# A fused gated-recurrence and two-layer kernel: moving first-unit copies between engines and merging the chunk-decay exponentials

## The chip, the cores and the metric

The kernel runs on one core of one Trainium2 chip. The metric is the device time of one execution in microseconds (us), as the median of several executions. The core has five engines with queues of their own: TensorE (PE, matmuls), VectorE (DVE), ScalarE (ACT), GpSimd (POOL) and SyncE (SP, which here only issues transfers), and 16 DMA engines. Each engine works through its own queue in order and waits on semaphores. In what follows, "Z", "X", "W", "H" and "O" are tensors in PSUM, the memory into which TensorE writes.

## The reference

First a gated linear recurrence over 768 tokens, for 4 batches and 8 heads of width 48; then a two-layer network on the 3072 resulting rows of 384 numbers, with a squared ReLU between its layers.

```python
def _attn_ref(q, k, v, alpha):                 # all (4, 8, 768, 48), float32
    state = np.zeros((B, H, D, D))
    for t in range(S):
        state = alpha[:, :, t, :, None] * state + np.einsum('bhd,bhde->bhde', k[:, :, t], v[:, :, t])
        y[:, :, t] = np.einsum('bhd,bhde->bhe', q[:, :, t], state)

def _moe_ref(x, w_in, w_out):                  # (3072, 384), (384, 2048), (2048, 384)
    r = np.maximum(x @ w_in, 0.0)
    return (r * r) @ w_out

x = attn_out.transpose(0, 2, 1, 3).reshape(B * S, H * D)
```

## The kernel before

The sequence is cut into chunks of 256 tokens; a chunk of one batch is a **unit**. There are 12 units, and units 0 to 3 are the first chunks of the four batches. A unit goes through these steps:

- **front**: load alpha, k, q and v; take logarithms of alpha on ScalarE; sum them along the tokens with a triangular matrix on TensorE; exponentials of the sums and of their negatives (ScalarE) give the decays `EQ` and `EK`; VectorE multiplies q and k by them (`QKS`); the result is transposed (`KQT`), for units 0 to 2 by TensorE through PSUM, and from unit 3 on by a transfer. The values are cast to bfloat16 (`VBF`).
- **kv** and **state**: products of keys and values (TensorE), masked to a head's own block (`SMD`), and carried to the next chunk with the chunk's decay (`SBD`).
- **p** (scores, 32 small matmuls), a mask (`PM`, VectorE), and **y** (output of the unit); then a copy to bfloat16 (`XBF`), a transpose (`XT`), and the two-layer network: first layer (`s1`, 48 matmuls of 256 columns in eight groups of six), ReLU, square, second layer (`s2`, 32 matmuls of 384 columns).

The instructions are not written in queue order. The kernel records operations with a priority (`prio`), a modelled cost and, where there is a choice, alternatives (`alts`) on another engine. A list scheduler in the same file then picks engine and order when the program is built. So a change of a number changes the order in all queues. Where the modelled TensorE queue has a hole ahead of the first second-layer matmul, `fill` puts matmuls of zeros there, into a bank whose content nobody reads.

The parts that the change touches (cuts are marked with `...`):

```python
    # which load is issued behind which (gates)
    AFTER = {(1, "v"): (0, "q"), ("win", 0): (1, "a"), ("win", 1): (1, "a"), 2: ("win", 0), ("wout", 0): ("win", 1),
             ("wout", 1): (2, "k"), 3: ("wout", 0)}
    ...
    # unit 0 only: front in two halves of four heads
    add("act", ... activation(ACM[la][:, 4 * x:4 * x + 4], bank[:, HD:HD + 4], AF.Exp), ..., name=f"ec{x}_{g}")
    add("pool", lambda e: e.tensor_copy(vout, vin), 830, p0 + 900, reads=[("raw", r, 3)], writes=[("vbf", vb)],
        name=f"vc{g}", alts={"act": (lambda e: e.activation(vout, vin, AF.Copy), act_ns(2 * HD))})
    ...
    add("dve", lambda e, to=to, at=at: e.tensor_copy(to, at), dve_ns(512, 2), px + 3000 + a, reads=psk,
        writes=[("kqt", kt, a, x)], name=f"et{a}{x}_{g}",
        alts={"act": (lambda e, to=to, at=at: e.activation(to, at, AF.Copy), act_ns(512))})
    ...
    # units 2 to 11: decays of pairs of tokens
    add("act", ... e.activation(EK[la][:, 1, :], psW[:, 0:HD], AF.Exp, scale=-1.0), ..., name=f"ei{g}")
    add("act", ... e.activation(EQ[la][:, 1, :], psW[:, 0:HD], AF.Exp), ..., name=f"ea{g}")
    if not last:
        add("act", ... e.activation(ACM[la][:], psW[:, HD:HD + H], AF.Exp), ..., name=f"ec{g}")
    ...
    # state: mask to the head's own block (first chunks), then the decay to the next chunk
    if first:
        add("dve", lambda e: e.tensor_tensor(sm3, hd(ps0), own, ALU.mult), dve_ns(HD), p0 + 2900,
            reads=[key0, ("own",)], writes=[("smd", x2)], name=f"sa{g}")
    ...
    if not last:
        acm = bcast(ACM[la], H, [[1, H], [0, D]])
        add("dve", ... tensor_tensor(TMP[1][:], ps1, SMD[x2][:], ALU.add), ..., name=f"sc{g}")
        add("pool", ... tensor_tensor(hd(SBD[sw][:]), hd(TMP[1][:]), acm, ALU.mult), ..., name=f"sd{g}",
            alts={"dve": ...})
```

Of the kernel before, what the change touches and what calls it, by code (L numbers as in the profile page):

```python
# [321 lines left out]
def act_ns(n):  # L322
    return 180 + n * 0.8333


def dve_ns(n, rate=1.0):
    return 150 + n / 0.96 / rate
# [6 lines left out]
def bass_gla_recurrent__then__act_relu_squared_kernel(  # L334
# [22 lines left out]
    FRONT = {0: 0, 1: 15124, 2: 28243, 3: 27962, 4: 36918, 5: 52460}  # L357
    ATTN = {1: 12619, 2: 26150, 3: 37152, 4: 50460}
    DENSE = {0: 20223, 1: 32105, 2: 46275, 3: 57124, 11: 158500}
    POOL_LOADS = {1: "v", 2: "akqv"}  # L360
# [16 lines left out]
    EQ = sb("eq", [128, 2, HD], FP32, 2)  # L377
    EK = sb("ek", [128, 2, HD], FP32, 2)
    ACM = sb("acm", [128, H], FP32, 2)
# [23 lines left out]
    OWN = nc.alloc_sbuf_tensor("own", [128, H], BF16)  # L403
    ZERO = nc.alloc_sbuf_tensor("zero", [128, 512], BF16)
# [40 lines left out]
    for buf, key in ((HSEL, "hsel"), (HCOL, "hcol"), (OWN, "own")):  # L445
        add("dve", fill(buf[:], 0.0), 100, -2e6, writes=[(key,)])
    for part, key, val in ((HSEL[0:1, 64:128], "hsel", -1000.0), (HSEL[32:33, 0:64], "hsel", -1000.0),
                           (HCOL[0:1, 0:H:2], "hcol", 1.0), (HCOL[32:33, 1:H:2], "hcol", 1.0),
                           (OWN[0:64, 0:H:2], "own", 1.0), (OWN[64:128, 1:H:2], "own", 1.0)):
        add("dve", fill(part, val), 100, -2e6, reads=[(key,)], writes=[(key,)])  # L450
# [20 lines left out]
    def weight(lay, w):  # L471
        cut = slice(w * FS * 128, (w + 1) * FS * 128) if lay == 0 else slice(w * FS, (w + 1) * FS)
        if lay == 0:
            src, dst = moe_w_in.rearrange("(kk p) n -> p kk n", p=128)[:, :, cut], WIN[:, :, cut]
        else:
            src = moe_w_out[w * FS * 128:(w + 1) * FS * 128, :].rearrange("(p e) n -> p (e n)", e=FS)
            dst = WOUT[:, cut, :].rearrange("p e n -> p (e n)")
        key = ("win", "wout")[lay]
        load_op[key, w] = add("pool", lambda e: e.dma_start(dst, src), 930, W_PRIO[lay] + w, writes=[(key, w)], name=f"{key}{w}",
                              dma=f"{key}{w}", lag=8600 / WS,  # L480
                              after=[load_op[AFTER[key, w]]] if (key, w) in AFTER else [])

# [4 lines left out]

    def named(x):
        return next(o for o in pr.ops if o.name == x)

    BEHIND = {"a": "ln", "k": "tr0_", "q": "tr1_", "v": "tr1_"}

    def load(g):
        b, i = units[g]
        t0 = i * T
        p0 = g * P
        r, la, qs, kt, pm, vb, x2 = (g % n for n in (NRAW, 2, NQKS, NKQT, NPM, NV, 2))
        first, last = i == 0, i == NST - 1
        sr, sw = 2 * b + i % 2, 2 * b + (i + 1) % 2

        for x in range(2) if g in BY_HEADS else ():
            hs = slice(4 * x, 4 * x + 4)
            src = alpha[b, hs, t0:t0 + T, :].rearrange("h (p j) d -> p h (j d)", j=2)
            dst = RAW[r][:, 0, hs].rearrange("p h j d -> p h (j d)")
            add("sp", lambda e, dst=dst, src=src: e.dma_start(dst, src), 600, L_PRIO[g] + x * 0.5,  # L505
                writes=[("raw", r, 0, x)], name=f"lda{x}_{g}", dma=f"a{r}{x}", lag=615)
        for j, t, nm in ((0, alpha, "a"), (1, k, "k"), (2, q, "q"), (3, v, "v"))[g in BY_HEADS:]:
            src = t[b, :, t0:t0 + T, :].rearrange("h (p j) d -> p h (j d)", j=2)
            dst, key = RAW[r][:, j], ("raw", r, j)
            ring, cost, gate = "sp", 600, AFTER.get((g, nm), AFTER.get(g))  # L510
            if nm in POOL_LOADS.get(g, ""):
                ring, cost = "pool", 930
            dst = dst.rearrange("p h j d -> p h (j d)")
            load_op[g, nm] = add(ring, lambda e, dst=dst, src=src: e.dma_start(dst, src), cost, (L_PRIO[g] + j if ring == "sp" else W_PRIO[2] + 10 * g + j),  # L514
                writes=[key], name=f"ld{nm}{g}", dma=f"{nm}{r}{ring}", lag=1230,
                after=([load_op[gate]] if gate else []) + ([named(f"{BEHIND[nm]}{g - 1}")] if g >= 5 else []))

    def front_by_heads(g, p0):
# [4 lines left out]
        def lanes(t, x):  # L523
            return t[la][:].rearrange("p j (x n) -> p j x n", x=2)[:, :, x]

        for x in range(2):
# [25 lines left out]
            add("act", lambda e, x=x, sums=sums: e.activation(lanes(EK, x), sums, AF.Exp, scale=-1.0), act_ns(HD),  # L552
                px + 500, reads=key, writes=[("ek", la, j, x) for j in range(2)], name=f"ei{x}_{g}")
            add("act", lambda e, x=x, sums=sums: e.activation(lanes(EQ, x), sums, AF.Exp), act_ns(HD),
                px + 510, reads=key, writes=[("eq", la, j, x) for j in range(2)], name=f"ea{x}_{g}")
            add("act", lambda e, x=x, bank=bank: e.activation(ACM[la][:, 4 * x:4 * x + 4], bank[:, HD:HD + 4], AF.Exp),
# [4 lines left out]
            name=f"vc{g}", alts={"act": (lambda e: e.activation(vout, vin, AF.Copy), act_ns(2 * HD))})  # L561

        for x in range(2):
            hs = slice(4 * x, 4 * x + 4)
            px = p0 + 40 * x
            for a, E, nm in ((0, EK, "ek"), (1, EQ, "eq")):
                add("dve", lambda e, a=a, E=E, hs=hs, x=x: e.tensor_tensor(
                    QKS[qs][:, a, :, hs, 0:D], RAW[r][:, 1 + a, hs].rearrange("p h j d -> p j h d"),
                    lanes(E, x).rearrange("p j (h d) -> p j h d", h=4), ALU.mult), dve_ns(HD), px + 1500 + 10 * a,
                    reads=[("raw", r, 1 + a, x), (nm, la, 0, x), (nm, la, 1, x)], writes=[("qks", qs, a, x)], name=f"{nm}m{x}_{g}")  # L570
            for a in range(2):
                bank, psk = psZ[:, a, :].bitcast(BF16), [("ps", "Z", a)]

                def tr(pe, a=a, bank=bank, hs=hs):
# [11 lines left out]
                add("dve", lambda e, to=to, at=at: e.tensor_copy(to, at), dve_ns(512, 2), px + 3000 + a, reads=psk,  # L586
                    writes=[("kqt", kt, a, x)], name=f"et{a}{x}_{g}",
                    alts={"act": (lambda e, to=to, at=at: e.activation(to, at, AF.Copy), act_ns(512))})

    def decays_by_token(g, p0, r, la):  # L590
# [22 lines left out]
        add("act", lambda e: e.activation(EQ[la][:], bank[:, 0:2, 0:HD], AF.Exp), act_ns(2 * HD), p0 + 510,  # L613
            reads=keys, writes=[("eq", la, 0), ("eq", la, 1)], name=f"ea{g}")
        add("act", lambda e: e.activation(ACM[la][:], bank[:, 0, HD:HD + H], AF.Exp), act_ns(8), p0 + 520,
            reads=keys, writes=[("acm", la)], name=f"ec{g}")

    def decays_by_pair(g, p0, r, la, last):
# [11 lines left out]
        def m1(incl):  # L630
# [15 lines left out]
        add("act", lambda e: e.activation(EQ[la][:, 1, :], psW[:, 0:HD], AF.Exp), act_ns(HD), p0 + 510,  # L646
            reads=[("ps", "W")], writes=[("eq", la, 1)], name=f"ea{g}")
        if not last:
            add("act", lambda e: e.activation(ACM[la][:], psW[:, HD:HD + H], AF.Exp), act_ns(8), p0 + 520,
                reads=[("ps", "W")], writes=[("acm", la)], name=f"ec{g}")  # L650
# [4 lines left out]
        if g < RATIO:  # L655
            add("pe", m1(False), pe_ns(1, HD), p0 + 530, reads=[("lab", la), ("lstr",)], writes=[("ps", "W")],
                name=f"m1s{g}")
            add("act", lambda e: e.activation(EQ[la][:, 0, :], psW[:, 0:HD], AF.Exp), act_ns(HD), p0 + 540,
                reads=[("ps", "W")], writes=[("eq", la, 0)], name=f"es{g}")
            add("pool", lambda e: e.tensor_tensor(hd(EQ[la][:, 0, :]), hd(EQ[la][:, 0, :]), al(0), ALU.mult), pool_ns(HD),  # L660
                p0 + 800, reads=[("eq", la, 0), ("raw", r, 0)], writes=[("eq", la, 0)], name=f"aq{g}",
                alts={"dve": (lambda e: e.tensor_tensor(hd(EQ[la][:, 0, :]), hd(EQ[la][:, 0, :]), al(0), ALU.mult),
                              dve_ns(HD))})
            return
# [5 lines left out]
        add("act", lambda e: e.activation(EQ[la][:, 0, :], LA1[la][:], AF.Exp), act_ns(HD), p0 + 540,  # L670
            reads=[("la1", la)], writes=[("eq", la, 0)], name=f"es{g}")

    def front(g):
# [19 lines left out]
        for a, E, key in ((0, EK, "ek"), (1, EQ, "eq")):  # L693
            add("dve", lambda e, a=a, E=E: e.tensor_tensor(  # L694
                QKS[qs][:, a, :, :, 0:D], RAW[r][:, 1 + a].rearrange("p h j d -> p j h d"),
                E[la][:].rearrange("p j (h d) -> p j h d", h=H), ALU.mult),
# [85 lines left out]
    def state(g, alone=True):  # L782
# [10 lines left out]
        if first:  # L793
            add("dve", lambda e: e.tensor_tensor(sm3, hd(ps0), own, ALU.mult), dve_ns(HD), p0 + 2900,
                reads=[key0, ("own",)], writes=[("smd", x2)], name=f"sa{g}")
# [6 lines left out]
        if not last:  # L802
            acm = bcast(ACM[la], H, [[1, H], [0, D]])
            add("dve", lambda e: e.tensor_tensor(TMP[1][:], ps1, SMD[x2][:], ALU.add), dve_ns(HD),  # L804
                p0 + 3600, reads=[key1, ("smd", x2)], writes=[("tmp", 1)], name=f"sc{g}")
# [175 lines left out]
    W_PRIO = (-5e5, -4e5, -4.5e5)  # L981
    ORDER = ["f0", "k0", "p0", "f1", "y0", "p1", "k1", "y1", "f2", "p2", "k2"]
    for g in range(3, G):
        ORDER += [f"f{g}", f"w{g - 1}", f"p{g}"]
    ORDER += [f"y{G - 1}"]
    AFTER = {(1, "v"): (0, "q"), ("win", 0): (1, "a"), ("win", 1): (1, "a"), 2: ("win", 0), ("wout", 0): ("win", 1),
             ("wout", 1): (2, "k"), 3: ("wout", 0)}
    AFTER.update({g: (g - 1, "q") for g in range(4, G)})
    load(0)
    load(1)  # L990
    for w in range(WS):
        weight(0, w)
    load(2)
    for w in range(WS):
        weight(1, w)
    for st in ORDER:
        kind, g = st[0], int(st[1:])
        if kind == "f":
            if g > 2:
                load(g)  # L1000
# [41 lines left out]
```

## Time and profile before

The median of three executions is 179.0 us (178.62 to 179.14). The profiled execution has a span of 177.2 us; times below are from its start.

| What | Value | Where it is read |
|---|---|---|
| TensorE granted clock | 1.0 | result of the profiled run |
| VectorE, ScalarE, GpSimd busy | 121.1, 120.0, 26.2 us | page, part 1 |
| first-layer matmuls | 576, on the chain 38% of the span | page, parts 5 and 4 |
| second-layer matmuls | 368 of 384 columns and 32 of 192 | page, part 5, and the chain |
| matmuls of zeros | 72, of which 65 ahead of the first first-layer matmul | page, part 5; groups of 0 to 18.46 us |
| first first-layer matmul | 18.46 us | chain, timeline |
| last matmul ends | 174.77 us | chain |

The page has six parts. Part 1 sums the busy time of each engine; part 2 cuts the span in 40 slices and gives the busy share of each in tenths; part 4 is the chain that ended last, followed backwards from the last instruction, so its shares say what the time was spent on; part 5 lists groups of instructions with the mean of one; part 6 lists transfers. A TensorE that shows as busy isn't necessarily doing useful work: the matmuls of zeros count as busy, and so does a matmul that overlaps its neighbour. For that reason the prediction reads TensorE from the chain, where each piece is given once, and not from the busy sum.

### The profile page before, as it was taken

To read this page: it belongs to the slowest core of one execution; us is meant where nothing else is said; L and a number is where in the kernel's file an instruction comes from. 1 tells how busy PE (TensorE), PEld (TensorE's weight loads), DVE (VectorE), ACT (ScalarE), POOL (GpSimd) and SP (SyncE) were. 2 spreads that over 40 slices of the span, in tenths; PEclk is the share of its full clock that TensorE was granted. 3 is DMA by queue.
4 is the path that set the end of the run, shared out by engine and by line. 5 is a ranking of instruction groups with operands and counts; after the bars stand their busy time and mean duration, and the time that the engine had idled before them with its cause. 6 is when DMAs were issued, how large, how long until landed. Compare 5 with 4: busy or idle time off the path is not lost.

```text
span 177.2 us, 5228 instructions
## 1 busy us (share of the span) xinstructions
PE 171.5 (97%) x2287; PEld 136.4 (77%) x2287; DVE 121.1 (68%) x197; ACT 120.0 (68%) x211; POOL 26.2 (15%) x35
## 2 busy tenths in 40 slices
PE   7799999999999999999999999999999999999994
PEld 5677798866788688688778777788787797798773
DVE  6479689699958977869949947748848647352130
ACT  5565489577779785758778758857887564475541
POOL 3160845120010204001102110200100200000000
PEclk9999999999999999999999999999999999999999
DMA  4999999999999799799989998699979930110112
GB/s 120 293 308 193 248 310 209 247 253 275 194 245 243 195 171 220 220 193 217 248 196 221 197 285 202 136 279 164 221 196 267 153 89 4 44 48 0 44 48 89
DMA packets 74615, 33.18 MB, mean 187 GB/s; under 512 B 69888, under 2 KB 73088, under 8 KB 74592
## 3 DMA queue, kind: packets, MB, share of 16 engines
q1 hardware_dynamic: 72944, 27.73, 68.0%
q0 software_dynamic: 1648, 5.11, 12.7%
q8 instruction: 18, 0.29, 0.7%
q14 instruction: 5, 0.04, 0.1%
HBM read 25.17 MB, written 4.72 MB: 169 GB/s over the span
## 4 chain that ended last, share of the span: by engine, by line
PE 88%; DMA 7%; SPq 2%; issue 1%; ACT 0%
PE psWH L930 38%; PE psO L966 34%; DMA win<-in_moe_w_in_dram 4%; PE psX L771 3%; DMA raw<-in_alpha_dram 3%; PE psX L764 3%; PE psX L827 2%; PE psZ L744 2%; SPq L514 2%; PE psX L900 1%; PE psZ L827 1%; PE psWH L632 1%; PE psX L873 1%; PE psZ L708 1%; SPq L505 1%
## 5 line engine op out<-in xcount | busy, mean ns | idle before, releaser
L930 PE MATMUL psWH<-xt,win 128*128 128x256 bf16 x576 | 74.5, 275 | 0.3 <-DMA win<-in_moe_w_in_dram 0.3
L930 PEld LDWEIGHTS psWH<-xt,win 128*128 128x128 bf16 x576 | 65.0, 145 | 5.4 <-DVE kqt L715 0.5
L966 PE MATMUL psO<-wout,gt 128*128 128x384 bf16 x368 | 69.0, 326 | 0.1
L938 ACT ACTIVATE rr<-psWH 128x512 bf16<-128x512 f32 x85 | 50.4, 595 | 26.0 <-PE psWH L930 24.8
L966 PEld LDWEIGHTS psO<-wout,gt 128*128 128x128 bf16 x368 | 35.3, 98 | 17.8 <-ACT osb L973 0.3
L948 DVE TENSOR_TENSOR gt<-rr 128x1024 bf16<-128x1024 bf16 (+1 forms) x43 | 24.2, 572 | 20.0 <-ACT rr L938 19.7
L973 ACT ACTIVATE osb<-psO 128x384 f32<-128x384 f32 x20 | 9.8, 491 | 11.6 <-PE psO L966 11.0
L952 ACT ACTIVATE gt<-rr 128x1024 bf16<-128x1024 bf16 (+1 forms) x17 | 15.8, 932 | 0.7
L840 DVE TENSOR_TENSOR pm<-psX,caus 128x1024 bf16<-128x1024 f32 x12 | 14.6, 1216 | 2.1 <-PE psZ L827 2.1
L840 DVE TENSOR_TENSOR pm<-psZ,caus 128x1024 bf16<-128x1024 f32 x12 | 14.6, 1215 | 1.6 <-PE psZ L827 1.6
L858 ACT ACTIVATE xbf<-psX 128x768 bf16<-128x768 f32 x11 | 8.9, 811 | 6.1 <-PE psZ L744 4.7
L797 DVE TENSOR_TENSOR tmp<-psZ,sbd 128x384 f32<-128x384 f32 x8 | 4.5, 557 | 11.5 <-PE psZ L744 11.4
L1010 PE MATMUL psO<-zero 128*128 128x256 bf16 x72 | 11.0, 301 | 1.3 <-DVE zero L426 1.3
L690 POOL CAST vbf<-raw 128x768 bf16<-128x768 f32 x6 | 5.4, 907 | 41.5 <-DMA raw<-in_v_dram 41.5
L694 DVE TENSOR_TENSOR qks<-raw,eq 128x768 bf16<-128x768 f32 x11 | 10.5, 952 | 0.6 <-POOL eq L660 0.3
L694 DVE TENSOR_TENSOR qks<-raw,ek 128x768 bf16<-128x768 f32 x11 | 10.4, 949 | 0.1
L1010 PEld LDWEIGHTS psO<-zero 128*128 128x128 bf16 x72 | 7.4, 108 | 2.7 <-DVE zero L426 1.3
L940 DVE TENSOR_SCALAR rr<-psWH 128x512 bf16<-128x512 f32 x11 | 7.5, 685 | 1.7 <-PE psWH L930 1.6
L806 POOL TENSOR_TENSOR sbd<-tmp,acm 128x384 bf16<-128x384 f32 x4 | 4.2, 1048 | 18.6 <-DVE tmp L804 18.6
L771 PE MATMUL psX<-vbf,pm 64*128 64x48 bf16 x384 | 6.9, 180 | 0.0
L653 DVE TENSOR_TENSOR ek<-ek,raw 128x384 f32<-128x384 f32 x9 | 6.0, 667 | 0.9 <-ACT ek L644 0.7
L625 POOL TENSOR_TENSOR prd<-raw 128x384 f32<-128x384 f32 x3 | 3.0, 1011 | 21.7 <-DMA raw<-in_alpha_dram 21.7
(120 smaller groups left out, 166.2 us busy)
## 6 DMA issues: line engine op xcount, KB each, us to landing
out_dram<-osb SPq DMA_DIRECT2D x23, 192.0 KB, 2.7
raw<-in_k_dram SPq DMA_DIRECT2D x11, 384.0 KB, 4.5
raw<-in_q_dram SPq DMA_DIRECT2D x11, 384.0 KB, 4.8
raw<-in_v_dram SPq DMA_DIRECT2D x10, 384.0 KB, 5.2
raw<-in_alpha_dram SPq DMA_DIRECT2D x10, 384.0 KB, 4.2
win<-in_moe_w_in_dram POOLq DMA_DIRECT2D x2, 768.0 KB, 9.2
wout<-in_moe_w_out_dram POOLq DMA_DIRECT2D x2, 768.0 KB, 9.0
raw<-in_v_dram POOLq DMA_DIRECT2D x2, 384.0 KB, 6.1
```

What stands on the lines that cost most here:

```text
L694: add("dve", lambda e, a=a, E=E: e.tensor_tensor(QKS[qs][:, a, :, :, 0:D], RAW[r][:, 1 + a].rearrange("p h j d -> p j h d"), E[la][:].rear ...
L771: ins = pe.matmul(psX[:, c, h * D:(h + 1) * D], PM[pm][64 * c:64 * c + 64, n // 2, rr_, n % 2, jk, :], VBF[vb][64 * c:64 * c + 64, h, jk, ...
L840: add("dve", lambda e, hf=hf, psT=psT: e.tensor_tensor(PM[pm][:, hf].rearrange("p r n j t -> p (r n) (j t)"), psT[:, :, :].rearrange("p r ...
L858: add("act", lambda e: e.activation(XBF[x2][:], psX[:, :, 0:HD], AF.Copy), act_ns(2 * HD), p0 + 6100, reads=[("ps", "X", 0), ("ps", "X", 1 ...
L930: ins = pe.matmul(psH[hb][:, i * T:(i + 1) * T], WIN[:, kk, hidden(fj)], mov, start=(kk == 0), stop=(kk == KT - 1))
L938: add("act", lambda e, hb=hb, rr=rr: e.activation(rr, psH[hb], AF.Relu), act_ns(512), pu + 600, reads=[("ps", "H", hb)], writes=[("rr", rb ...
L940: alts={"dve": (lambda e, hb=hb, rr=rr: e.tensor_scalar(rr, psH[hb], 0.0, None, ALU.max), dve_ns(512))})
L948: add("dve", lambda e, dst=dst, sq=sq: e.tensor_tensor(dst, sq, sq, ALU.mult), 148 + k * 267, pu + 1200, reads=[("rr", rb, h) for h in ran ...
L952: "act": (lambda e, dst=dst, sq=sq: e.activation(dst, sq, AF.Square), act_ns(k * 512))})
L966: ins = pe.matmul(psS, GT[gt][:, fj, j, :], WOUT[:, fj, :], start=(fj == 0), stop=(fj == FT - 1))
L973: add("act", lambda e, ob=ob, psS=psS: e.activation(OSB[ob][:], psS, AF.Copy), act_ns(DM), ps_ + 700, reads=[keyS], writes=[("osb", ob)], ...
L1010: pr.fill(lambda pe: pe.matmul(psO[:, 0:256], ZERO[:, 0:128], ZERO[:, 0:256], skip_group_check=True), 109, min(o.start for o in pr.order[" ...
```

## The change

What it does, part by part:

1. **Unit 0, transposed keys and queries.** The four copies `et` from PSUM get ScalarE as their first engine; the two of the keys have no alternative any more, the two of the queries may go to VectorE.
2. **Unit 0, values.** The cast `vc0` is left to GpSimd alone; before, the scheduler could pick ScalarE, and did.
3. **State of first chunks.** The mask `sa` gets an alternative on ScalarE: two activations with a 0/1 scale per partition (`HALF`), each for every second head, in place of one multiplication by `own`.
4. **Chunk decays.** The buffer `ACM` goes; the eight decays lie behind the 768 numbers of `EQ`. For units 2 to 7 the exponential of the sums `ea` runs over 392 columns in place of 384 and brings them along, so `ec` goes there.
5. **Priorities** of several units move (`FRONT`, `ATTN`, `DENSE`), and the state update `sc` of unit 0 comes later. The loads are recorded one by one with a table of gates (`GATE`); the gates are the same as before.

It is for a shorter way through the first units, and for less work on ScalarE.

```diff
-    FRONT = {0: 0, 1: 15124, 2: 28243, 3: 27962, 4: 36918, 5: 52460}
-    ATTN = {1: 12619, 2: 26150, 3: 37152, 4: 50460}
-    DENSE = {0: 20223, 1: 32105, 2: 46275, 3: 57124, 11: 158500}
+    FRONT = {0: 0, 1: 15467, 2: 23878, 3: 24800, 4: 40758, 5: 53978}
+    ATTN = {1: 13331, 2: 26488, 3: 40698, 4: 54378}
+    DENSE = {0: 22431, 1: 35061, 2: 46556, 3: 58580, 11: 159500}
+    GATE = {"v1": "q0", "win0": "a1", "win1": "a1", "a2": "win0", "k2": "win0", "q2": "win0", "v2": "win0",
+            "wout0": "win1", "wout1": "k2", "a3": "wout0", "k3": "wout0", "q3": "wout0", "v3": "wout0"}
...
-    EQ = sb("eq", [128, 2, HD], FP32, 2)
+    EQ = sb("eq", [128, 2 * HD + H], FP32, 2)
-    ACM = sb("acm", [128, H], FP32, 2)
...
         add("pool", lambda e: e.tensor_copy(vout, vin), 830, p0 + 900, reads=[("raw", r, 3)], writes=[("vbf", vb)],
-            name=f"vc{g}", alts={"act": (lambda e: e.activation(vout, vin, AF.Copy), act_ns(2 * HD))})
+            name=f"vc{g}")
...
-                add("dve", lambda e, to=to, at=at: e.tensor_copy(to, at), dve_ns(512, 2), px + 3000 + a, reads=psk,
+                add("act", lambda e, to=to, at=at: e.activation(to, at, AF.Copy), act_ns(512), px + 510 + a, reads=psk,
                     writes=[("kqt", kt, a, x)], name=f"et{a}{x}_{g}",
-                    alts={"act": (lambda e, to=to, at=at: e.activation(to, at, AF.Copy), act_ns(512))})
+                    alts={"dve": (lambda e, to=to, at=at: e.tensor_copy(to, at), dve_ns(512, 2))} if a else None)
...
-        add("act", lambda e: e.activation(EQ[la][:, 1, :], psW[:, 0:HD], AF.Exp), act_ns(HD), p0 + 510,
-            reads=[("ps", "W")], writes=[("eq", la, 1)], name=f"ea{g}")
-        if not last:
-            add("act", lambda e: e.activation(ACM[la][:], psW[:, HD:HD + H], AF.Exp), act_ns(8), p0 + 520,
-                reads=[("ps", "W")], writes=[("acm", la)], name=f"ec{g}")
+        n = HD if last else HD + H
+        add("act", lambda e: e.activation(EQ[la][:, HD:HD + n], psW[:, 0:n], AF.Exp), act_ns(n), p0 + 510,
+            reads=[("ps", "W")], writes=[("eq", la, 1)] + ([] if last else [("acm", la)]), name=f"ea{g}")
...
+            def by_head(e):
+                for x in range(2):
+                    ins = e.activation(sm3[:, x::2], hd(ps0)[:, x::2], AF.Copy, scale=HALF[:, x:x + 1])
+                return ins
+
             add("dve", lambda e: e.tensor_tensor(sm3, hd(ps0), own, ALU.mult), dve_ns(HD), p0 + 2900,
-                reads=[key0, ("own",)], writes=[("smd", x2)], name=f"sa{g}")
+                reads=[key0, ("own",), ("half",)], writes=[("smd", x2)], name=f"sa{g}",
+                alts={"act": (by_head, 2 * act_ns(HD // 2))})
...
-                p0 + 3600, reads=[key1, ("smd", x2)], writes=[("tmp", 1)], name=f"sc{g}")
+                p0 + (4300 if g == 0 else 3600), reads=[key1, ("smd", x2)], writes=[("tmp", 1)], name=f"sc{g}")
```

## The prediction

> **What bounds the kernel now.** I read the busy table first, then the chain that ended last, then TensorE's waits, and last the timeline of the stage that the change is about. The page says:
>
> ```profile
> PE 171.5 (97%) x2287; PEld 136.4 (77%) x2287; DVE 121.1 (68%) x197; ACT 120.0 (68%) x211; POOL 26.2 (15%) x35
> PE 88%; DMA 7%; SPq 2%; issue 1%; ACT 0%
> ```
>
> TensorE has 88% of the chain, VectorE and GpSimd don't appear, ScalarE rounds to nothing. So an instruction taken off ScalarE or VectorE is worth nothing by itself; it counts where TensorE waits for its result. The chain in order of time shows where TensorE takes over:
>
> ```profile
> 4.99 5.25 DMA raw<-in_alpha_dram
> 10.24 0.30 issue
> 10.54 7.78 DMA win<-in_moe_w_in_dram
> 18.32 0.14 issue
> 18.46 0.85 PE psWH L930 x6
> 19.31 0.35 PE psX L827 x16
> 19.66 0.22 PE psZ L827 x16
> 19.88 1.47 PE psWH L930 x12
> 21.35 0.45 PE psZ L744 x16
> 21.79 0.81 PE psWH L930 x6
> 22.60 0.44 PE psO L1010 x4
> ```
>
> Columns are start, length, what. Up to 18.46 us the chain is transfers: unit 1's alphas, and behind them, by a gate, the first half of the first layer's weights, which lands at 18.32. From 18.46 on it is TensorE. Two stages, then. In the first, four microseconds of compute more or less cost nothing as long as it ends before 18.32. In the second, every matmul in the queue counts. TensorE's own waits agree:
>
> ```profile
> PE psWH L930 <- DMA win<-in_moe_w_in_dram: 0.3, 1, 0.3
> ```
>
> That is its only wait after 18.4 us and up to 62 us of more than 0.1 us that the view names. The matmuls of zeros (L1010) fill what would be holes.
>
> [...] the windows of 4.43 to 18.46 us show a DMA share of 1.1, whichever queue issued. So the landing at 18.32 follows from bytes and gates, which the change leaves alone. [...] GpSimd's multiply at 29.73 us took 1.76 us, another 0.82. For the new cast on GpSimd this matters, below. [...] here 97% includes 72 matmuls of zeros.
>
> **The change part by part.**
>
> *Merged decays.* Six instructions `ec` of 0.18 us go (units 2 to 7), and `ea` grows by 8 columns: from 384 columns at 0.49 us and 8 at 0.18 us a column costs 0.8 ns, so 0.01 us each. Saved: 6 x (0.18 - 0.01) = 1.0 us of ScalarE. It idles about 57 of 177 us. On the path: 0, except that at unit 2 the bank W comes free 0.18 us sooner for the next sum.
>
> *Values on GpSimd.* The cast took 0.84 us on ScalarE from 9.09 us, and casts on GpSimd average 0.907. GpSimd issues unit 1's values until 8.15 + 1.09 = 9.24, so the cast runs 9.24 to 10.15. VectorE's two-input multiplies end at 8.93, so no conflict. The result comes 0.2 us later than 9.93, and kv0 moves from 9.98 to about 10.2. The cast stands in GpSimd's queue ahead of the weights' issue, but that waits for the alphas until 10.24 anyway: margin 0.1 us.
>
> *Keys and queries on ScalarE.* In the new order three of four copies are on ScalarE, 0.58 each. ScalarE ends its exponentials at 6.89; with the transposes at 7.35, 8.7 and 9.2 (nine and two matmuls of zeros between, 0.109 each), the copies end near 8.4, 9.65 and 10.25. VectorE loses two copies of 0.41 before the masks, and `sc` is put behind them. VectorE is then: `sa` 10.75 to 11.3, the last copy to 11.7, masks (1.21 each, one every 1.14) to 14.0 instead of 14.49, `sc` to 14.55, the multiplies of unit 1 again at 14.5 (they were at 14.41). So y0 starts near 14.15 instead of 14.81.
>
> *Unit 1.* Its first transposed copy moves to ScalarE (1.02 us for 1024) and VectorE does only the transposed `xt0` copy (0.56) and the second (0.68). Multiplies end at 16.4, `xt0` at 17.05, the second copy at 17.75 (18.29 before). Scores p1 can run 17.9 to 18.45, ahead of the first layer. And in the new order they do stand ahead of it, where the old one has six matmuls, then p1.
>
> *What that brings.* The scores are 0.35 + 0.22 = 0.57 us of TensorE. After them the next six first-layer matmuls take longer:
>
> ```profile
> 63.44 0.66 PE psWH L930 x6
> 72.94 0.81 PE psWH L930 x6
> ```
>
> The first stands behind a second-layer group, the other behind scores, so a return costs 0.15. Both, 0.72 us, leave the second stage for the time of the wait. From there I counted both orders to the end: 576 + 368 + 32 matmuls of the layers, the same attention groups, 24 returns before and 23 after. Matmuls of zeros behind the first first-layer matmul: 7 before, 9 after, so 2 x 0.109 = 0.22 back. Net: -0.72 + 0.22 = **-0.50**. The new start is p1's end plus a return, some 18.45 to 18.6, where it was 18.46: **+0.1**.
>
> *Waits of ScalarE's making.* In the new order the transposed `xt1` copy is on ScalarE (0.81), ahead of ln2 and a ReLU; the alphas of unit 2 land no sooner than 24.4. By hand from 22.6 on, groups 8 and 10 of the first layer wait 0.1 to 0.2 us for ReLUs, where the old ones waited for unit 2. At the second layer's start I get 31.25 instead of 32.16, and there the first output weights (issued 22.29, 8.9 us to landing) arrive at 31.2: just in time, no more to gain.
>
> *Later.* From 18.46 to 174.77 is 156.3 us. I added the pieces of the chain there, window by window: 67 us first layer, 61 and 2.7 second layer, 20 attention, 5 sums and transposes, 0.8 matmuls of zeros. That is the whole of it. One step leads off TensorE before the very end, behind the copy out of bank O:
>
> ```profile
> 36.61 1.31 PE psO L966 x8
> 37.94 0.50 ACT osb L973
> 38.49 0.82 PE psO L966 x4
> ```
>
> and even there kv2 runs inside the gap. So the second stage has nearly no wait to lose, only work to shed, while a new order can add waits. Total: -0.5 + 0.1 = -0.4 by counting; the walk by hand through 18 to 36 us, with its ReLU waits, has -0.75 at the end of the sixteenth first-layer group (35.85 for 36.60). I take -0.6 and choose **178.4**.
>
> **Rivals.**
> 1. *All hidden.* Only the weights' landing counts and the queue repays the rest in waits. For it: the chain has nothing of ScalarE, and the first stage ends by transfer. Against: p1 really leaves the second stage. It would make 179.0.
> 2. *GpSimd's cast holds up the weights.* If the values land later than 9.05, or the cast takes the 1.76 us seen once, the issue at 10.54 slips by up to 0.8, and everything behind it too. For it: a margin of 0.1. Against: the DMA engines are full until 18 us, so a late issue finds work queued ahead. It would make 179.0 to 179.8.
> 3. *ScalarE becomes the bound from 18 to 35 us.* It takes on the first state's mask (two of 192 elements, an estimate of 0.33 each from the slope above), copies of unit 1, `xbf` and `xt`. For it: eight ReLUs of 0.6 us for each 8 x 0.66 us of matmuls leave it little room. Against: VectorE takes squares in return (the order shows 12 squares on ScalarE in place of 17). It would make 179 to 180.
> 4. *More than counted.* The 0.77 us of zeros' matmuls and the half microsecond at bank O shrink too, because unit 2 comes sooner. Against: unit 2 hangs on loads that land at 24.4 and later. It would make 177.6.
>
> **Range and chances.** The sum gives 178.4; rivals 1 to 3 lie 0.6 to 1.6 above, rival 4 0.8 below, and executions spread by 0.5. Range 177.4 to 179.7. Two per cent are 3.6 us, more than any term: faster by over 2% 0.03, within 2% 0.95, slower by over 2% 0.02.
>
> **What would show it.** In the changed profile: first first-layer matmul at 18.4 to 18.6 us with p1 just ahead of it, the weights' issue at 10.5; 9 matmuls of zeros behind it; second layer's start near 31.3; last matmul ended near 174.2; ScalarE without six 8-column activations. I am wrong if the weights land later than 18.5, if TensorE shows waits on ScalarE of over 0.5 us in 18 to 40 us, or if TensorE's chain leads over other engines for more than 1 us behind 40 us.

## The result, and the profile after

The changed kernel took 179.97 us (median of four executions, 179.61 to 180.57), the kernel before 179.07 beside it: a ratio of 1.0059, 95% interval 1.0033 to 1.0086. Predicted were 178.4 us, in a range up to 179.7: a gain of 0.6 came out as a loss of 0.9. The span of the profiled execution went from 177.2 to 178.2 us.

From the page after: the busy times (with the number of instructions), and the chain's shares by engine.

```profile
PE 171.6 (96%) x2286; PEld 136.2 (76%) x2286; DVE 118.1 (66%) x192; ACT 121.9 (68%) x215; POOL 27.9 (16%) x35
PE 78%; DMA 14%; SPq 2%; ACT 2%; issue 1%; POOL 0%; DVE 0%
```

TensorE's share of the chain fell from 88 to 78% and the transfers' rose from 7 to 14%. ScalarE became busier, not less (121.9 us for 120.0): it lost six short exponentials and took on copies and ReLUs (88 ReLUs for 85). The chain in order of time says where the transfers got in (start, length, what):

```profile
5.33 5.29 DMA raw<-in_alpha_dram
10.62 0.30 issue
10.91 0.75 POOL win L483
11.67 11.61 DMA win<-in_moe_w_in_dram
23.27 0.28 issue
23.56 8.47 DMA wout<-in_moe_w_out_dram
32.03 0.05 issue
32.08 0.82 PE psO L964 x4
...
41.84 0.57 DVE osb L973
42.41 0.03 issue
42.44 0.36 PE psX L756 x8
```

Before, the chain left the transfers at 18.46 us. Now it stays on them until 32.03: over the *second* half of the first-layer weights to the first half of the second-layer weights, which GpSimd issues only once that second half has landed. TensorE's timeline around the first layer (start, busy time, line, tiles, count; in brackets idle time and what ended it):

```profile
17.68 0.93 PE L1013 MATMUL psO<-zero 128*128 128x256 bf16 x7
18.62 0.42 PE L825 MATMUL psX<-kqt 64*64 64x128 bf16 x16
18.87 0.39 PE L825 MATMUL psZ<-kqt 64*64 64x128 bf16 x16
19.20 1.53 PE L928 MATMUL psWH<-xt,win 128*128 128x256 bf16 x12
```

The first layer starts 0.74 us later than before (18.46). Its weights landed 0.50 later (18.82 for 18.32), and unit 1's scores (L825), which stand ahead of it, ended later still.

In offsets to the kernel before, at the same piece of work: unit 1's scores -0.62 (they are now ahead of the first layer), unit 2's scores -0.57, unit 2's output +0.60 (the new order has six more first-layer matmuls, 0.66 us, between the two), unit 5's output +0.93, and +0.95 at the end.

### The profile page after: what moved, and what is told of

Its sections match the earlier page's. It is cut to its first block, busy times and chain, and to the rows that moved or that the text cites. A ratio compares the mean times of both kernels' runs of the same rounds, so it can differ in the third digit from the quotient of the medians.

```text
span 178.2 us, 5216 instructions
## 1 busy us (share of the span) xinstructions
PE 171.6 (96%) x2286; PEld 136.2 (76%) x2286; DVE 118.1 (66%) x192; ACT 121.9 (68%) x215; POOL 27.9 (16%) x35
## 4 chain that ended last, share of the span: by engine, by line
PE 78%; DMA 14%; SPq 2%; ACT 2%; issue 1%; POOL 0%; DVE 0%
PE psO L964 33%; PE psWH L928 31%; DMA win<-in_moe_w_in_dram 7%; DMA wout<-in_moe_w_out_dram 5%; DMA raw<-in_alpha_dram 3%; PE psX L763 3%; PE psX L756 2%; SPq L508 2%; PE psX L825 2%; PE psZ L736 2%; PE psX L898 1%; PE psZ L825 1%; ACT gt L950 1%; PE psWH L626 1%; ACT rr L936 1%
## 5 line engine op out<-in xcount | busy, mean ns | idle before, releaser
L936 ACT ACTIVATE rr<-psWH 128x512 bf16<-128x512 f32 x88 | 51.9, 595 | 24.3 <-PE psWH L928 22.9
L946 DVE TENSOR_TENSOR gt<-rr 128x1024 bf16<-128x1024 bf16 (+1 forms) x48 | 27.1, 572 | 23.1 <-ACT rr L936 22.8
L971 ACT ACTIVATE osb<-psO 128x384 f32<-128x384 f32 x22 | 10.8, 492 | 13.8 <-PE psO L964 13.4
L686 DVE TENSOR_TENSOR qks<-raw,eq 128x768 bf16<-128x768 f32 x11 | 11.7, 1067 | 0.8 <-ACT eq L662 0.5
L950 ACT ACTIVATE gt<-rr 128x1024 bf16<-128x1024 bf16 (+1 forms) x12 | 11.4, 950 | 0.3
L797 POOL TENSOR_TENSOR smd<-tmp,own 128x384 bf16<-128x384 f32 x4 | 3.8, 948 | 38.2 <-DVE tmp L795 38.2
L683 ACT ACTIVATE vbf<-raw 128x768 bf16<-128x768 f32 x8 | 6.7, 836 | 1.5 <-DMA raw<-in_v_dram 1.4
L938 DVE TENSOR_SCALAR rr<-psWH 128x512 bf16<-128x512 f32 x8 | 5.5, 690 | 2.3 <-PE psWH L928 2.2
L804 POOL TENSOR_TENSOR sbd<-tmp,eq 128x384 bf16<-128x384 f32 x4 | 4.8, 1200 | 12.4 <-DVE tmp L802 12.4
```

Source lines behind the costliest of these rows:

```text
L686: add("dve", lambda e, a=a, E=E: e.tensor_tensor(QKS[qs][:, a, :, :, 0:D], RAW[r][:, 1 + a].rearrange("p h j d -> p j h d"), E.rearrange(" ...
L936: add("act", lambda e, hb=hb, rr=rr: e.activation(rr, psH[hb], AF.Relu), act_ns(512), pu + 600, reads=[("ps", "H", hb)], writes=[("rr", rb ...
L946: add("dve", lambda e, dst=dst, sq=sq: e.tensor_tensor(dst, sq, sq, ALU.mult), 148 + k * 267, pu + 1200, reads=[("rr", rb, h) for h in ran ...
L950: "act": (lambda e, dst=dst, sq=sq: e.activation(dst, sq, AF.Square), act_ns(k * 512))})
L971: add("act", lambda e, ob=ob, psS=psS: e.activation(OSB[ob][:], psS, AF.Copy), act_ns(DM), ps_ + 700, reads=[keyS], writes=[("osb", ob)], ...
```

## The experiments

In most of them the queues are kept as the scheduler had made them for the changed kernel, and single operations are moved within them; so nothing else shifts. `move(a, b)` puts `a` ahead of `b` in its queue. Ratios are to the kernel before on the same chip.

**The same queues, nothing moved.**

> The changed kernel with its queues fixed as they are, so that later runs can move single instructions. Here nothing is moved. Theory A (the order is what costs: a late start of the first layer, a wait for unit 3's values at y2, three first-layer groups in a row): 180.0 us, first first-layer matmul at 19.0 to 19.3, y2 near 42.4, whatever the loads of unit 0 and 1 do. Theory B (the profiled run of the changed kernel happened to have late loads: unit 1's alphas at 10.62 for 10.24): the alphas land near 10.24 this time, the first first-layer matmul is at 18.7 or sooner, and the time is below 179.6.

179.06 us, ratio 0.9979 [0.9956, 1.0001]. The same program that lost 0.9 us lost nothing here. The profile starts a little earlier (alphas issued at 4.68 instead of 5.33 us), scores at 18.10, first layer at 18.67, second-layer weights landed at 30.94, no wait at unit 2's output; but TensorE waited 0.41 us for the second half of the first-layer weights. So executions differ, and one comparison of two profiles doesn't carry a verdict of half a microsecond.

**The first state's update ahead of the masks** (`move("sc0", "mk0_0")`).

> The changed kernel with one move: unit 0's state update sc0 stands ahead of the two masks in VectorE's queue again, so GpSimd's sd0 runs near 12.6 instead of 14.9 and no longer beside unit 1's two-input multiply. Theory A: the multiply eqm1 takes 0.95 instead of 1.58, scores p1 start some 0.3 sooner (the masks are then 0.55 later, y0 too), first layer near 18.9, and the end comes 0.2 to 0.3 sooner: 179.7. Rival (the landing of the weights sets the first layer's start): eqm1 shortens, the first layer still starts at 19.1 or later, 180.0.

179.29 us, ratio 0.9994 [0.9967, 1.0020]. VectorE's timeline in the changed kernel, and then in this run:

```profile
15.58 1.58 DVE L686 TENSOR_TENSOR qks<-raw,eq 128x768 bf16<-128x768 f32 x1
```

```profile
14.79 0.95 DVE L686 TENSOR_TENSOR qks<-raw,eq 128x768 bf16<-128x768 f32 x1
```

and GpSimd's state product, again first in the changed kernel:

```profile
14.89 1.46 POOL L804 TENSOR_TENSOR sbd<-tmp,eq 128x384 bf16<-128x384 f32 x1 [2.46 <-DVE tmp L802]
```

```profile
11.84 0.82 POOL L804 TENSOR_TENSOR sbd<-tmp,eq 128x384 bf16<-128x384 f32 x1
```

The change put `sc0` behind the masks, and its follower on GpSimd then runs beside unit 1's multiplication: both lose some 0.63 us. Apart, the scores begin at 17.82, 0.28 earlier than in the run above, an execution that had begun within 0.1 us of it. But the first layer now waits for its weights at 18.71 (0.25 us), so unit 1's output is where it was (22.08 us, and 22.04 in the run above). The cost is real, and behind it stands the landing.

**Unit 3's values loaded ahead of its queries** (`move("ldv3", "ldq3")`).

> The changed kernel with one move: unit 3's values are loaded ahead of its q. Theory A (y2 and kv3 stand in one block, which waits for the cast of unit 3's values, and these land at 41.5): y2 starts at 41.8 to 41.9 instead of 42.44 and the end comes 0.5 to 0.6 sooner: 179.4. Rival (the copy out of bank O, which the profile names as the end of that wait, holds TensorE): y2 stays at 42.4, 180.0. Second rival: q now lands too late and the gain at y2 is lost at unit 3's scores.

179.72 us, ratio 1.0026 [1.0002, 1.0049]. Unit 2's output has no wait (offset -0.12 to the kernel before), but by unit 3's output that is +0.85. The queries are issued later, unit 4's loads are gated behind them, and its values reach their cast on ScalarE only at 49.11 (48.73 in the changed kernel's first profile). A ReLU stands behind that cast, and TensorE waits 0.70 us for it. One wait for a transfer was exchanged for another.

**Two of the three first-layer groups in a row** (`move("s1_4_0", "s2_3_1_0")`).

> The changed kernel with one move: the first first-layer group of unit 4 stands ahead of the four second-layer groups behind unit 5's scores, as in the kernel before, so that two groups follow on each other there and not three. Theory A (the third group waits for the ReLU of the first, as there are two H banks): the distance from those scores to the next y shrinks from 5.57 to 5.29 us, and the end comes 0.28 sooner: 179.7. Rival (later waits take it back): 180.0.

180.61 us, ratio 1.0086 [1.0064, 1.0107]: a miss. TensorE's timeline there:

```profile
74.11 0.88 PE L928 MATMUL psWH<-xt,win 128*128 128x256 bf16 x6 [1.11 <-DMA xt<-xbf]
74.82 2.77 PE L964 MATMUL psO<-wout,gt 128*128 128x384 bf16 x16
77.42 0.82 PE L928 MATMUL psWH<-xt,win 128*128 128x256 bf16 x6
78.66 0.88 PE L928 MATMUL psWH<-xt,win 128*128 128x256 bf16 x6 [0.42 <-ACT rr L936]
```

The group put ahead waits 1.11 us for unit 4's transposed tokens, and the last one still waits for a ReLU. The kernel before could have this order because it had unit 4's output earlier (65.33 us, and 67.35 here, with unit 5's scores at 72.30 and 72.36).

**The change once more, unaltered.**

> The changed kernel, instruction for instruction as first measured (179.97 against 179.07), once more in five rounds; its twin with the same queues gave 179.06 against 179.12. Theory A (the landings of loads differ from execution to execution by half a microsecond and more, and the first comparison drew late ones): 179.0 to 179.5, ratio to the kernel before within 0.3%. Theory B (the order costs 0.9 us): 180.0, ratio 1.005.

179.43 us, ratio 1.0023 [1.0000, 1.0047]. The start is late here (alphas issued 6.11, first layer 19.51), and the end is only 0.55 behind the kernel before.

**The merged exponentials alone,** in the queues of the kernel before (the short one of units 2 to 7 taken out).

> The kernel before with its queues fixed as they are; only the six small exponentials of units 2 to 7 go and the one ahead of each runs over 392 columns. Theory A (ScalarE isn't on the path): the time of before, within 0.2 us; ScalarE's busy time 1.0 us lower. Rival (ScalarE's ReLUs come sooner and TensorE with them): 0.3 us faster or more.

179.85 us, ratio 1.0027 [0.9999, 1.0056]; ScalarE has 205 instructions for 211. No gain, as reckoned; the 0.5 us more are over the 0.2 expected, but the interval still holds 1.

**A third of the first-layer and a quarter of the second-layer weights loaded,** in both kernels; the multiplications use what is loaded in place of the rest. That leaves out most of the weights' traffic, not TensorE's work.

```diff
-src, dst = moe_w_in.rearrange(...)[:, :, cut], WIN[:, :, cut]
+src, dst = moe_w_in.rearrange(...)[:, 0:1, cut], WIN[:, 0:1, cut]
```

> The kernel before with the same queues, but a third of the first layer's weights and a quarter of the second layer's are loaded and read in place of the rest (it leaves the other weights out of the computation; matmuls are as many and as large). Theory A: the first layer starts at 17.8 to 18.0, when unit 0's rows and the matmuls of zeros ahead are done, instead of 18.46, and the time is 178.5.

> The changed kernel with the same cut of the weights' loads. Theory A (what the changed order loses, it loses to landings): scores p1 and then the first layer start at 18.5 to 19.1, set by unit 1's multiply; no wait for values at y2; by the count of work (-0.50) and this start (+0.6 to +1.1 against before with the same cut) the time is 0.0 to 0.5 above that one. Rival B (ScalarE's new copies hold TensorE in 18 to 40 us): 0.9 or more above it.

177.75 us, ratio 0.9926 [0.9900, 0.9951], for the kernel before, and 178.69, 0.9968 [0.9950, 0.9986], for the changed one. With these landings out of the way the change still loses 0.9 us, more than the 0.0 to 0.5 expected. Unit 0's scores and the start of the first layer, in the kernel before and then in the changed one:

```profile
10.57 0.42 PE L828 MATMUL psX<-kqt 64*64 64x128 bf16 x16
17.63 0.82 PE L931 MATMUL psWH<-xt,win 128*128 128x256 bf16 x6
```

```profile
11.32 0.42 PE L826 MATMUL psX<-kqt 64*64 64x128 bf16 x16
19.31 1.53 PE L929 MATMUL psWH<-xt,win 128*128 128x256 bf16 x12
```

In these two profiles the end differs by 1.31 us, and 0.75 of that is a later start of the second execution (unit 0's scores). Counted from there, the first layer starts 0.93 later, since unit 1's scores stand ahead of it, and what follows is 0.37 shorter: 0.56 is lost. The view of waits names none of TensorE's behind 18 us, so it isn't the hold by ScalarE that the rival named.

**The first unit's values cast on ScalarE again.**

> The changed kernel's queues, with one move: the cast of the first unit's values goes back from GpSimd to ScalarE, ahead of unit 1's exponentials. Theory: the cast has nothing to do with the weights' landings; GpSimd still waits 0.6 to 1.3 us for the second half of the first-layer weights before it issues the first half of the second-layer weights, the time is the changed kernel's within 0.3 us or up to 0.5 us longer where ScalarE's exponentials of unit 1 come later. Rival: the cast on GpSimd is what holds the transfers up; then that wait is gone as in the kernel before (0 to 0.1 us), unit 3's values land about half a us earlier, and the time falls by about 0.5 us.

179.52 us, ratio 0.9982 [0.9961, 1.0002]. GpSimd's wait is gone, as the rival had it, but not because the weights came sooner: the second half landed 11.5 us after its issue (11.6 with the cast on GpSimd), and the first half 8.5 after (7.9), which held up the loads that GpSimd issues in between. The cast isn't shown to be the cause.

**The kernel before, its queues kept.**

> The kernel before with its own queues, fixed, nothing changed: a second look at its landings. Theory (landings differ between executions, whatever the kernel): a time within 0.3 us of the kernel before, and the landings of the four halves of the weights up to 0.7 us from the first look (18.32 for the first half, 31.2 for the third). Rival (the changed order causes the late landings): no wait of GpSimd ahead of the third half here either, and that half within 13.0 us of the first.

178.93 us, ratio 0.9974 [0.9953, 0.9994]. The same instructions as the kernel before lie 0.26% under it, and their interval leaves out 1: an interval here doesn't cover what differs from one build or set of executions to the next. GpSimd had no wait for the second half, and the second layer's first half landed 12.5 us after the first layer's first half, as the rival had it.

**Six first-layer matmuls ahead of the scores again** (`move("s1_0_0", "p0_1")`).

> The changed kernel's queues, with the first six first-layer multiplications again ahead of unit 1's key-query multiplications, as in the kernel before. Theory (moving those 32 multiplications ahead of the first layer gains nothing, since they end after the weights have landed): the first layer starts at the landing or at 18.5 to 18.8 instead of 19.2, and the end comes 0 to 0.4 us earlier than in the changed kernel, none of it lost. Rival (the prediction's step): they lay in idle time and go back onto the path, so the end comes 0.5 to 0.7 us later.

179.94 us, ratio 1.0019 [0.9990, 1.0047]. The ratio is the changed kernel's (1.0021 in the mean of its four), so no gain is shown. The end of the profiled execution, one of the longer ones, came 0.68 us later than in the changed kernel's first profile, where I had expected up to 0.4 earlier. Two things did it:

```profile
19.47 0.90 PE L928 MATMUL psWH<-xt,win 128*128 128x256 bf16 x6 [1.16 <-DMA win<-in_moe_w_in_dram]
...
22.28 0.52 PE L736 MATMUL psZ<-vbf,qks 64*128 64x96 bf16 x16 [0.53 <-DVE pm L838]
```

The weights landed 8.79 us after their issue, 0.9 more than in the changed kernel's first profile (7.91), and 1.16 us of TensorE lay idle that the scores could have filled; and the scores, now later, hand on 0.53 us through their mask. In this execution it would have paid to have them ahead.

**The three groups parted by four second-layer matmuls** (`move("s1_4_0", "s2_3_1_3")`, the same for `s1_4_1`).

> The changed kernel's queues, with the three first-layer groups in a row at 76 us parted: four second-layer multiplications go between the second and the third. Theory: the 0.28 us that the third waited for its ReLU go, and nothing else moves; the time falls by 0.2 to 0.3 us. Rival: the first of them now waits for the transposed tokens of the fourth unit, as it did when it went ahead by sixteen; then up to 0.9 us is added at that place.

180.30 us, ratio 1.0047 [1.0023, 1.0072]: another miss, but not by the rival's reason. ScalarE's timeline:

```profile
78.69 0.49 ACT L971 ACTIVATE osb<-psO 128x384 f32<-128x384 f32 x1 [3.03 <-PE psO L964]
79.08 0.59 ACT L936 ACTIVATE rr<-psWH 128x512 bf16<-128x512 f32 x1
```

In ScalarE's queue the copy of the second layer's result (L971) stands ahead of the ReLU (L936). It waited for the four matmuls that I had put in between, and the ReLU behind it: the third group waited 1.07 us instead of 0.28. (This profile also held unit 2's output 1.55 us for late values, so only the piece at 76 us is read.)

**Both kernels unaltered, side by side.**

> The changed kernel once more, unaltered, beside the kernel before on the same chip. Theory (the change costs nothing that lasts; executions differ in when the weights land): a ratio between 0.998 and 1.004. Rival (the loss of the first measurement is the change's): 1.005 to 1.008. In the profile, either way, the wait ahead of the sixth unit's state product is the 0.28 us of the three groups in a row, since that does not depend on landings.

> The kernel before compared with itself on the same chip: how far two builds of one program lie apart. Theory: the ratio is within 0.003 of 1, though not always within its own interval, and this profile's landings are again up to 0.7 us from the first look's. Rival: within 0.001, and then differences of 0.002 to 0.006 elsewhere belong to the kernels.

The change: 180.18 us, ratio 1.0021 [0.9988, 1.0055]. The kernel before against itself: 180.13, ratio 1.0007 [0.9973, 1.0040]. That is the number of the second rival, but with its interval, and with 0.9974 in the run above of the kernel before, it doesn't show that differences of 0.002 belong to the kernels. TensorE in the first (a wait for the second half of the first-layer weights), then in the second (the wait ahead of the first layer):

```profile
23.20 1.50 PE L928 MATMUL psWH<-xt,win 128*128 128x256 bf16 x12 [0.38 <-DMA win<-in_moe_w_in_dram]
```

```profile
19.11 0.82 PE L930 MATMUL psWH<-xt,win 128*128 128x256 bf16 x6 [0.88 <-DMA win<-in_moe_w_in_dram]
```

**Both waits that were found, removed** (`move("sc0", "mk0_0")`, `move("s1_4_2", "s1_4_3")`).

> The changed kernel's queues with two moves: the first state's update goes ahead of unit 1's masks on VectorE, so that GpSimd's product no longer runs beside VectorE's two-input multiplication, and the third of the three first-layer groups goes behind the sixth state product. Theory: the first takes 0.3 us off unit 1's path but hands it to the landing of the first weights, the second takes 0.2 to 0.28 us off at 77 us and keeps it; the end is 0.2 to 0.5 us earlier than the changed kernel's, a ratio of 0.996 to 1.000 to the kernel before. Rival: the sixth state product is not ready when the group no longer stands ahead of it, and the 0.28 us come back there as a wait; then nothing is gained.

180.61 us, ratio 1.0039 [1.0011, 1.0068]. At unit 5's output it is 0.85 us ahead of the kernel before: 0.66 of that is the group that now comes later, and the wait there is gone. At unit 6's scores it is 0.46 behind. The group that was moved makes three in a row again, behind unit 5's output, where a copy of 0.81 us stands ahead of the ReLUs in ScalarE's queue: given back at once, and more.

**Light weights, first layer ahead of the scores.** Loads cut as above, with `move("s1_0_0", "p0_1")`.

> The changed kernel's queues with two thirds of the first-layer and three quarters of the second-layer weights left unloaded (the multiplications use the loaded part in their place), and six first-layer multiplications put back ahead of unit 1's key-query multiplications. Without that move the end was 0.94 us above the kernel before with the same cut. Theory (both pieces lie on TensorE's path once no landing holds the first layer, so their order is worth nothing in itself): within 0.3 us of the run without the move, unless the masks then come late for unit 1's values, which costs up to 0.6 us more. Rival (the prediction: the key-query multiplications ahead of the first layer fill idle time): 0.6 to 0.8 us longer with no wait added on TensorE.

179.24 us, ratio 0.9989 [0.9967, 1.0011]. In the profile the end is 0.04 earlier than in the changed kernel with the same cut, with a start 0.63 earlier; so the move costs 0.59. Of this 0.53 is the mask's wait:

```profile
20.65 0.51 PE L737 MATMUL psZ<-vbf,qks 64*128 64x96 bf16 x16 [0.53 <-DVE pm L839]
```

That wait is this run's own: it has six first-layer matmuls between the scores and the product that needs the mask, the kernel before has twelve. For the order of scores and first layer in itself 0.06 is left, from one execution of each.

## Why the prediction was wrong

Cut every profile where the prediction did, at the first first-layer matmul. "Landed" is the first half of the first-layer weights, the second stage goes from that matmul to the last 32 matmuls, and the last column is GpSimd's wait for the second half of these weights.

| Execution | landed | first stage ends | second stage | GpSimd's wait |
|---|---|---|---|---|
| before: first, `e10`, `e14` | 18.32, 18.42, 18.75 | 18.46, 18.55, 19.11 | 153.47, 153.21, 153.24 | none |
| change: first, `e1`, `e5`, `e13` | 18.82, 18.30, 19.41, 18.34 | 19.20, 18.67, 19.51, 18.58 | 153.68, 153.18, 152.97, 153.75 | 0.88, 1.32, 0.58, 1.16 |
| light (`e7`, `e8`): before, change | 15.37, 15.87 | 17.63, 19.31 | 153.09, 152.72 | none |

Means: first stage 18.71 before and 18.99 with the change (+0.3; predicted +0.1), second stage 153.31 and 153.40 (+0.1; predicted -0.50). Together +0.4 us, 0.2%, which the ratios repeat: 1.0059, 0.9979, 1.0023 and 1.0021 for the change (mean 1.0021), 0.9974 and 1.0007 for the kernel before against itself. So what is shown is a gain that did not come. Of the 0.9 us of the first measurement no more than some half is the change's, as far as these few executions tell; what made the rest is open.

- **Two stages: right for the kernel before, not for the new order.** With the change the transfers carry the chain to 32.03 in the first profile and to 23.19 in `e1`.
- **Merged decays, 0 on the path:** `e6` shows no gain.
- **Values on GpSimd: right.** The cast ran 9.62 to 10.45, before the alphas landed at 10.62; rival 2 falls.
- **Copies on ScalarE: right.** Unit 0's output came at 14.51, for 14.81 before, in an execution whose loads were issued 0.34 later (predicted 14.15).
- **Unit 1: wrong.** I had its multiplications end at 16.4 and the scores at 17.9; they were 17.16 and 18.62. The multiplication lost 0.63 in the collision with GpSimd, which I had made possible myself by reading that `sc0` goes behind the masks: I looked for a conflict with the cast only. At the scores the collision is worth 0.28 (`e2`). About 0.3 is the later start.
- **First layer +0.1: far off in the first profile, close in the mean.** It measured +0.74: the landing came 0.50 later, 0.37 of it because the weights were issued later, and the scores added 0.24. From landing to first layer it took 0.14, 0.13 and 0.36 us before and 0.38, 0.37, 0.10 and 0.24 with the change, so the scores ahead cost little there. But they were free only where TensorE would have waited for the weights. That wait was 0.25 us in the first profile (0.3 in my fence), 0.71 in `e10` and 0.88 in `e14`, each behind six matmuls of zeros (0.65 us). In the four executions the scores began 0.20, 0.20, 0.48 and 0.33 us ahead of the landing, so a part of them was hidden. In the light runs, where no landing holds the first layer, it starts 0.93 later.
- **-0.50 in the second stage, with "nearly no wait to lose": the step that failed.** The work is shed: in the light runs the second stage is 0.37 shorter, with 0.28 of new wait inside. The old order had no wait to lose, but I wrote that a new order can add waits and put in 0.1 to 0.2 us of them up to 36 us and none behind. With the weights loaded in full the stage came out 0.1 longer in the mean, not 0.50 shorter. The new waits that the profiles show, below, are about 0.7 us in the mean of the four, close to the 0.6 that is missing; between single executions both differ by more than that mean.

The first new wait is in all four executions. From unit 5's scores to its output the same work, 18 first-layer and 16 second-layer matmuls, takes 5.29 us in the kernel before and 5.57 or 5.58 in each of the four, here in the kernel before and in `e1`. Three first-layer groups follow each other there, and the third waits 0.28 us for its ReLU:

```profile
72.30 0.42 PE L827 MATMUL psX<-kqt 64*64 64x128 bf16 x16
72.88 0.88 PE L930 MATMUL psWH<-xt,win 128*128 128x256 bf16 x6
73.59 2.76 PE L966 MATMUL psO<-wout,gt 128*128 128x384 bf16 x16
76.19 1.47 PE L930 MATMUL psWH<-xt,win 128*128 128x256 bf16 x12
77.59 0.36 PE L764 MATMUL psX<-sbd,kqt 128*64 128x96 bf16 x8
```

```profile
71.92 0.42 PE L825 MATMUL psX<-kqt 64*64 64x128 bf16 x16
72.57 2.77 PE L964 MATMUL psO<-wout,gt 128*128 128x384 bf16 x16
75.18 2.38 PE L928 MATMUL psWH<-xt,win 128*128 128x256 bf16 x18
77.49 0.36 PE L756 MATMUL psX<-sbd,kqt 128*64 128x96 bf16 x8
```

The others differ between executions. The wait for the second half of the first-layer weights was 0.41 us in `e1` and 0.38 in `e13`, that for the first half of the second-layer weights 0.16 in the first profile. Unit 2's output was held 0.64 us in the first profile and 0.17 in `e13`; `e5` has none of these. TensorE's timeline in the first profile names the copy out of bank O, but the page's waits of the weight loads name the reason, and `e3` took the wait away:

```profile
PEld psX L756 <- ACT vbf L683: 1.0, 1, 1.0
ACT vbf L683 <- DMA raw<-in_v_dram: 1.4, 2, 0.8
```

Unit 3's values landed late, their cast was late (it began at 41.55 us, after 0.82 us of waiting for them), and unit 2's output stands in one block with unit 3's products. I had put the second-layer weights at 31.2 from the landing before; that held for `e1` (30.94), not for the first profile (32.03). Of the signs that I had named, one came in the first profile: the weights landed later than 18.5.

Rival 1, all hidden at 179.0, came nearest. Still open: why in these four executions of the new order, and in none of the three of the old one, GpSimd waited for the second half. It landed 11.6 to 12.1 us after its issue against 10.7 to 11.2. One of the 16 pieces in which it lands made the difference: the other fifteen were there 10.9 to 11.1 us after the issue, against 10.5 to 11.1. Neither the cast (`e9`) nor the late state product (`e2`, which waited 0.60 too) explains it. The other runs that load all weights in the changed order have 11.5 to 12.0, but `e15` 11.0; whether the order causes it is not shown.

## What to carry to other kernels

Work moved ahead of a wait for a transfer was free here only up to the time that TensorE idled there (0.25 to 0.88 us in the kernel before) or spent on filling work (0.65), not up to the length of the transfer (7.78 to 8.20); read it from the waits, in several executions. A count of work shed is a gain only after the waits of the new order are taken off (here 0.50 us counted, and some 0.7 of new waits). When an order changes, list the pairs that newly run at the same time on VectorE and GpSimd (one cost each side 0.63 or 0.64 us here), and what stands ahead of each ReLU in its queue (in `e12` a copy there made TensorE wait 1.07 us). A shift of 0.3% needs both kernels profiled more than once before any piece of it is given a cause: the same changed program came out at 1.0059 and at 0.9979.

## What the hardware showed that was not expected

- VectorE's multiplication of two SBUF inputs (768 columns) took 0.95 us alone (`e2`) and 1.58 beside GpSimd's of 384, which went from 0.82 to 1.46: both sides pay, 0.63 and 0.64 us. The multiplication ahead of it, which had begun before GpSimd's (14.71 against 14.89), still took 0.95.
- The same issue of unit 0's values by SyncE took from 1.55 us (`e3`) to 3.04 (`e5`); unit 0's output came at 13.98 where it took 1.61 (`e1`) and at 14.82 in `e5`. It hits both orders: in `e6`, which has the old one, it took 3.02.
- The landing of one and the same half of the first-layer weights came 7.78, 8.20 and 8.15 us after its issue in the three executions of the kernel before, and 8.79 in `e11`, whose order treats it alike; so it doesn't follow from bytes and gates alone, as the prediction had it.
